# Batch 0 of a packed-attention and ELU-FFN kernel, done by head groups

## The chip, the cores and the metric

The program runs on one core of one Trainium2 chip. The metric is the device time of one execution, in microseconds (us). Engines are named as the profile names them: PE (TensorE matmul; PEld its weight loads), DVE (VectorE), ACT (ScalarE), POOL (GpSimd) and SP (SyncE, which here only issues DMAs). Times of day in this document are us from the start of the profiled execution's span.

## What is computed

```python
def sm_attn(qq, kk, vv):
    s = scale * np.matmul(qq, kk.transpose(0, 1, 3, 2))
    s = s - np.max(s, axis=-1, keepdims=True)
    a = np.exp(s)
    a = a / (np.sum(a, axis=-1, keepdims=True) + 1e-09)
    return np.matmul(a, vv)
p_packed = sm_attn(p, k, v)
out = sm_attn(q, p_packed, p_packed)
...
h = x @ w_in
g = np.where(h > 0.0, h, alpha * (np.exp(np.minimum(h, 0.0)) - 1.0))
return (g @ w_out).astype(np.float32)
```

There are 8 batches, 8 heads, 576 tokens, 64 columns a head, 32 packed queries a head, and x is the attention's output with the heads side by side (4608 x 512). w_in is 512 x 2048, w_out 2048 x 512, all float32.

## The kernel before, in words

**The work of a batch.** The first attention (packed queries p against k) gives 32 packed values a head. The kernel never forms x: since x is A times the packed values, with A the weights of the second softmax, h is A times M, where M is the packed values times w_in. Heads are kept in two groups g: the even heads (g = 0) lie in partitions 0 to 63 of the inputs, the odd ones (g = 1) in 64 to 127, and four heads of 32 packed queries fill 128 rows. A batch runs through `attention`: scores `s1`, maximum and exponential (`smax1`, `sexp1`), transposes `tr1` and copies out of PSUM, the sums with the values `pv`, division `norm`, a transpose `tr2` whose copy `tr2c` leaves the packed values in `ppT`, then for each of two cuts of the tokens the second softmax: scores `s2`, and on DVE `fold` (a 32x32 transpose), `smax`, `ssub`, (ACT `sexp`), `ssum`, `srec` (two small instructions), `smul`, `unfold`. Batch 0 is cut at token 256; its first cut is called the first stretch here.

**M and the products.** `mstep` multiplies `ppT` by 512 columns of w_in in two parts of 256 columns (M part 0 needs blocks 0 and 1 of w_in, part 1 blocks 2 and 3), and ACT or DVE copies the part out of PSUM. A product f (line 1536 for batch 0's first four) multiplies one block of 128 columns of M by the weights A, summed over the two groups; ACT takes it through `relu` and `ex`, DVE through `elu`, `cast` and `sub_own` split it in a high and a low half, and `out_mm` (lines 1658 to 1661) multiplies it by block f of w_out. After these first products PE goes on to products of the same kinds to the end.

**Weights.** Each block of 128 columns of w_in (called i0, i1, ...) or rows of w_out (o0, o1, ...) is loaded by SP as 512 KB, then `top` (a cast on ACT or DVE) and `join` (DVE) turn the loaded words into their float32 form; for w_out `high` and `low` split it further.

**What sets the order.** All work is collected as operations with their dependences. The order in which they are issued, and the engine of each (A, V, G for ACT, DVE, POOL), is written out in a table of numbers, `ORDER`; `PLACES` gives the PSUM banks. Every engine works through its instructions in that order, and one that waits holds up those behind it on its engine. All loads go through SP's one queue. `ONES` gives, by operation, how many extra matmuls (`warm_up`, line 435, on a tile of ones, results unused) PE does behind it; they come to an end before the first product.

Of the kernel before, what the change touches and what calls it, by code (L numbers as in the profile page):

```python
# [10 lines left out]
F32 = mybir.dt.float32  # L11
# [14 lines left out]
0 2 1 7 8 9 10 11 403 404V 405 406V 14 12 416 417V 17 15A 16A 3 4 20 18A 19A 21 13 23A 22A 24 25A  # L26
418 408 5 26 409V 410 400 401A 27 28 29 6 37 48 424 30 425A 402 411 31 32 33 34 529 530A 747 38 39
407G 55 35A 426 412A 413 754 531 748 755 749 40 49 50 56 532A 750 756 751A 414V 757 415G 752G 57 761
41 59 42 758A 759G 43 36 44 419 420A 58 421 753 62 762 763 432 60 65 422V 760 433A 63A 64A 764 768
440 441A 434 442 533 765A 766V 51 61 66A 67V 45 423G 769 534 535 52 770 771 68 69A 435 436A 772V  # L30
773V 775 782 70A 71 437 776 783 767 438V 777 778 72A 551 784 793 427 428A 552 456 439V 785 779A 780G
457A 786A 53 429 430A 431G 557 553 73 794 795 558 458 801 74 75 554 443 444A 787V 796 76 445 802 803
774 797 448 449A 781 450 798V 799G 451 559 77 804 446A 555 447G 806 807A 808G 78 556 810 811 812 813
814 560 561 46A 818 819 820 79 459 788 800 562 80 821 47 54 95 102 789A 805 81 815A 816G 823 84 791A
85 822 452A 453 536 537 824A 827 828 460A 825G 86 87 454A 835 836 837 461 829 455G 840 831 809 830
491 96 817 826 838 538 88 89 832A 833G 82A 83 462A 841A 844 845 90 842V 91 92 504 846 97 852 848 847
463G 505A 499 506 834 843 103 93A 853 94 865 854 492A 849V 850G 855 857 104 858A 106 872 851 866 867
# [12 lines left out]
1013 573 1011 1038A 1045A 115 117A 656G 657G 574 116V 1039V 1046V 658V 540 665V 666G 1031 1048 1049  # L50
1055 1027 1040 1056 1057 1058 1050 655 100 101 142 1051 1032 1062 1069 1052A 663V 664G 659A 660V
1059V 1005 1028 1053V 1063 1060G 1064 1047 1054 1070 1065 661V 662V 667 1066A 1067G 1061 1071 1072
1076 1083 1073A 1074G 1068 1029 1077 1084 1030 669V 1078 541 548 1085 670G 1086 654 1079 549 671V
1080V 1087A 542 543 550 1033 544 1081G 676A 678A 679G 681 677V 672V 118 119A 1088V 1075 673G 1096
1097 1104 120 143 1098 1100 674A 1099 675G 1090 131 1101A 1102G 1113 1082 1105 668 1114 1106 1115
121 122 123 124 125 1109 1089 1103 1110A 144 682G 1107 1116 1117 683V 1118A 1108 1119V 1111V 1121
1122 1123 1124 1130 1126 1127A 684V 689V 1128V 691V 1112 1120 1131 1132 1133 1134 685A 686V 1138
1091 687A 1125 1139 1140 1143 1141 1129 1135A 1136V 1144V 1093 1094 1095 1145G 1147 1155 126 690G
1148 1137 1146 1149 1156 1151 1157 1160 1150 1158 1092 1152A 1153V 127 128 1170 132 133 1161A 1159
1142 688G 1162G 692G 1171 1172 1173 1178 1179 1180 1181 680 1174 1175A 1154 1163 1183 1167 1184A  # L60
1187 1195 695V 1176V 1188 1189 1164 1177 134 1185V 1191 1190 1196 1186 1192A 696G 1182 1168 1169
1193G 1165 1166 1224 697V 698V 135 704V 1197 1200 1194 705G 707 1198 1199 1201A 1204 1212 1202V 1203
1205 1206 699V 700V 701V 1208 1207 1213 1214 1217 1215 1209A 1210V 1218A 1219G 1227 1234 1211 136
137 1228 1229 1230 1241 1235 1236 1237 1220 149 1231A 1232V 1233 138 139 1238A 694 1239G 1242 1243
1244 1225 1248 1245A 1246V 693 702V 703V 708V 709V 1249 706 1250 1251 1255 1256 710V 1257 1258 1252A
1253G 1221 1222 1223 1240 1247 715A 716V 1259A 1260V 717A 711A 712V 713A 714V 719 1262 1269 718V
1283 575 578 1263 1264 1265 721V 722G 720 1270 1271 1226 1272 576 577 1266A 1267V 1276 723V 129A
730A 1254 1261 130 731V 733 728A 729V 724A 725V 726A 727V 581 732 1273A 1274V 734V 579 1289 1286
1268 1275 1277 1278 1279 735G 580 736V 140A 1280A 1281V 737V 1298 738G 1313 582 583 1290 1304 743A
744V 739A 740V 1291 741A 742G 150 152 1292 746 153 154 745 156 157 1305 151 1282 1319 155 1287 584  # L70
1306 1307 1293G 1294G 1284 1295G 1296 1297 1334 1320 141 158 1308V 1309V 1310G 1321 1322 1323V 1324V
1325V 1311 1312 1299 159 162 1326 1327 1335 1336 1337 1338G 145 1339G 1328 1300 1301 1302 1303 1340G
160 1314 164 1349 1315 1316 1343 1350 1317 1318 1351 1352 1353G 1354G 585 1330 1331 586 1355V 1332
1341 1342 1356 1364 1288 1365 1357 1366 1329 1333 1367 1368V 1369V 1370G 1379 1380 1381 1382 1383V
1345 163 1346 1344 1347 1348 1360 1358 1361 165 146 1384V 1385V 1371 1372 1386 1387 1394 1395 166
167 1416 1396 161 1417 1418 1397 1420 1398G 1419 1362 1399V 168 169A 1359 1363 1375 1400V 1421 1373
1388 1401 170V 171 172A 1216 1402 1422 1423 1424 1426 1438 1439 1440 1441 1427G 1428V 1376 1377 1443
1374 1378 1442 1444 1445 1448 1446 147 148 173 1429G 1430 1449G 1450G 174 175 176 1285 1425 1431
# [116 lines left out]
    "623476764764674507501234454664670460126723064647676765045614653204545465456450456120457365777777"  # L195
    "7777032105674333330"
)
ONES = {0: 3, 8: 8, 17: 4, 21: 3, 24: 2, 26: 16, 529: 7}


@with_exitstack
def packed_attention_elu_ffn(
# [22 lines left out]
    nc = tc.nc  # L225
# [1590 lines left out]
```

## Time and profile before

| | us |
|---|---|
| three timed runs | 641.54, 643.30, 643.62 |
| their median | 643.3 |
| the profiled execution | 642.62 |
| its span, first to last instruction | 640.8 |
| PE busy in it | 630.3 |
| DVE busy in it | 534.7 |
| ACT busy in it | 418.9 |
| POOL busy in it | 164.9 |

The profiled execution's time holds 1.8 us around its span. Busy times are of one engine each, and PE's includes the matmuls on ones before the first product.

### The profile page before, as it was taken

To read this page: it belongs to the slowest core of one execution; us is meant where nothing else is said; L and a number is where in the kernel's file an instruction comes from. 1 tells how busy PE (TensorE), PEld (TensorE's weight loads), DVE (VectorE), ACT (ScalarE), POOL (GpSimd) and SP (SyncE) were. 2 spreads that over 40 slices of the span, in tenths; PEclk is the share of its full clock that TensorE was granted. 3 is DMA by queue.
4 is the path that set the end of the run, shared out by engine and by line. 5 is a ranking of instruction groups with operands and counts; after the bars stand their busy time and mean duration, and the time that the engine had idled before them with its cause. 6 is when DMAs were issued, how large, how long until landed. Compare 5 with 4: busy or idle time off the path is not lost.

```text
span 640.8 us, 16120 instructions
## 1 busy us (share of the span) xinstructions
PE 630.3 (98%) x6130; PEld 561.9 (88%) x6130; DVE 534.7 (83%) x1093; ACT 418.9 (65%) x796; POOL 164.9 (26%) x258
## 2 busy tenths in 40 slices
PE   9999999999999999999999999999999999999996
PEld 4567988889789888999989897999889998999996
DVE  3999988779999789878886998898788989667756
ACT  3789987566677657755776577656566667545452
POOL 1224223433232311222123232123111322113121
PEclk9999999999999999999999999999999999999999
DMA  9985795656489978887888989888877777565762
GB/s 346 374 279 197 246 320 166 230 158 225 143 296 307 277 240 280 286 299 231 297 277 276 269 264 317 271 296 301 252 267 272 224 217 245 170 201 189 230 195 82
DMA packets 85405, 160.43 MB, mean 250 GB/s; under 512 B 24272, under 2 KB 40144, under 8 KB 85200
## 3 DMA queue, kind: packets, MB, share of 16 engines
q1 hardware_dynamic: 85040, 158.88, 75.3%
q8 instruction: 48, 0.79, 0.5%
q10 hardware_dynamic: 288, 0.52, 0.2%
q14 instruction: 29, 0.24, 0.1%
HBM read 132.90 MB, written 26.48 MB: 249 GB/s over the span
## 4 chain that ended last, share of the span: by engine, by line
PE 85%; DVE 5%; DMA 5%; ACT 1%; issue 1%; POOL 1%; SPq 0%; DVEq 0%; POOLq 0%; ACTq 0%
PE psum L1426 37%; PE psum L1271 20%; PE psum L1543 6%; PE psum L998 4%; PE psum L1658 4%; PE psum L1661 4%; PE psum L1659 4%; PE psum L435 2%; PE psum L815 2%; DMA kvq<-in_qT 2%; DMA swb<-swb_dram 2%; PE psum L876 1%; DMA out<-part 1%; PE psum L1536 1%; DVE part L1458 1%
## 5 line engine op out<-in xcount | busy, mean ns | idle before, releaser
L1353 POOL TENSOR_TENSOR w<-w 128x128 f32<-128x128 f32 (+1 forms) x167 | 93.8, 565 | 298.5 <-DVE w L1278 77.7
L428 ACT CAST g<-w 128x896 fp32r<-128x896 f32 x96 | 90.0, 940 | 61.2 <-POOL w L1353 28.7
L1361 DVE TENSOR_TENSOR g<-w,g 128x896 fp32r<-128x896 f32 x96 | 104.6, 1092 | 16.6 <-ACT g L428 15.6
L1271 PE MATMUL psum<-a_hi,m_hi 128*128 128x256 f32 (+1 forms) x384 | 112.5, 293 | 0.0
L1271 PE MATMUL psum<-a_lo,m_hi 128*128 128x256 f32 (+1 forms) x384 | 110.2, 287 | 0.0
L1271 PE MATMUL psum<-a_hi,m_lo 128*128 128x256 f32 (+1 forms) x384 | 110.2, 287 | 0.0
L1426 PE MATMUL psum<-wo_b,g 128*128 128x256 f32 x672 | 94.2, 276 | 0.0
L1426 PE MATMUL psum<-wo_a,g 128*128 128x256 f32 x672 | 93.8, 276 | 0.0
L1426 PE MATMUL psum<-swa,g 128*128 128x256 f32 x672 | 93.5, 275 | 0.2 <-DMA swa<-swa_dram 0.2
L1426 PEld LDWEIGHTS psum<-wo_b,g 128*128 128x128 f32 x672 | 84.3, 192 | 4.8 <-issue 4.0
L1426 PEld LDWEIGHTS psum<-wo_a,g 128*128 128x128 f32 x672 | 84.3, 192 | 3.1 <-issue 1.3
L1426 PEld LDWEIGHTS psum<-swa,g 128*128 128x128 f32 x672 | 84.4, 192 | 0.4 <-DMA swa<-swa_dram 0.4
L1271 PEld LDWEIGHTS psum<-a_hi,m_hi 128*128 128x128 f32 x384 | 73.2, 191 | 9.5 <-issue 2.8
L1271 PEld LDWEIGHTS psum<-a_lo,m_hi 128*128 128x128 f32 x384 | 73.3, 191 | 0.1
L1271 PEld LDWEIGHTS psum<-a_hi,m_lo 128*128 128x128 f32 x384 | 73.2, 190 | 0.0
L1283 ACT ACTIVATE e<-psum 128x320 f32<-128x320 f32 x96 | 41.2, 431 | 31.9 <-PE psum L1271 31.3
L1426 PE MATMUL psum<-swb,g 128*128 128x256 f32 x336 | 56.5, 277 | 0.8 <-DMA swb<-swb_dram 0.6
L1426 PEld LDWEIGHTS psum<-swb,g 128*128 128x128 f32 x336 | 46.6, 192 | 3.4 <-issue 2.2
L1278 DVE SCALAR_TENSOR_TENSOR w<-e,psum 128x256 f32<-128x256 f32 x96 | 39.1, 414 | 9.8 <-ACT e L1286 8.4
L1286 ACT ACTIVATE e<-e 128x320 f32<-128x320 f32 x96 | 44.4, 470 | 2.5
L1353 DVE TENSOR_TENSOR w<-w 128x128 f32<-128x128 f32 (+1 forms) x121 | 40.8, 342 | 6.0 <-POOL w L1353 3.8
L1278 DVE SCALAR_TENSOR_TENSOR w<-w,psum 128x512 f32<-128x512 f32 x48 | 32.7, 683 | 13.7 <-ACT w L1286 12.2
(143 smaller groups left out, 1222.5 us busy)
## 6 DMA issues: line engine op xcount, KB each, us to landing
swa<-swa_dram SPq DMA_DIRECT2D x96, 512.0 KB, 5.0
swb<-swb_dram SPq DMA_DIRECT2D x96, 256.0 KB, 4.0
kvq<-in_v SPq DMA_DIRECT2D x16, 640.0 KB, 6.2
raw<-in_w_out SPq DMA_DIRECT2D x16, 511.8 KB, 5.5
raw<-in_w_in SPq DMA_DIRECT2D x16, 511.8 KB, 6.1
kvq<-in_kT SPq DMA_DIRECT2D x14, 576.0 KB, 6.2
kvq<-in_qT SPq DMA_DIRECT2D x14, 576.0 KB, 5.7
out<-part SPq DMA_DIRECT2D x28, 256.0 KB, 4.5
```

The costliest lines, as they stand in the source:

```text
L428: (nc.scalar.copy if e == "ACT" else nc.vector.tensor_copy)(out=out, in_=in_)
L998: nc.tensor.matmul(ps.t[cols_of(pair), g, :w], lhsT=st.ppT.t[rows_of(g), pair, :], rhs=w_in_sb[rows_of(g), pair, c * FC + part * w:c * FC ...
L1271: nc.tensor.matmul(ps, lhsT=m_b[p].t[:, g, o:o + P], rhs=in_turn(st.a.t[q][:, g, cols]), start=(n == 0), stop=(n == 3 * G - 1),)
L1278: nc.vector.scalar_tensor_tensor(out=out, in0=e_, scalar=-1.0, in1=ps, op0=ALU.add, op1=ALU.max)
L1283: nc.scalar.activation(out=out, in_=ps, func=AF.Relu, scale=-1.0)
L1286: nc.scalar.activation(out=x, in_=x, func=AF.Exp, scale=-1.0)
L1353: eng(e).tensor_tensor(out=out, in0=x, in1=y, op=o)
L1361: nc.vector.tensor_tensor(out=g_b.all[:, 7 * P:(7 + b1 - b0) * P], in0=blocks(b0, b1), in1=g_b.all[:, :(b1 - b0) * P].bitcast(F32), op=ALU ...
L1426: nc.tensor.matmul(a.t[:, at * H:(at + rhs.shape[1]) * H], lhsT=operand(blk, p), rhs=rhs, start=new and n == k == 0, stop=a.final == (u, m ...
L1543: nc.tensor.matmul(ps_b.t[:, :n_tok], lhsT=m_b[x].t[:, g, o:o + P], rhs=in_turn(st.a.t[y][:, g, cols]), start=(n == 0), stop=(n == 3 * G - 1),
L1658: nc.tensor.matmul(a.t, lhsT=g_b.t[0][:, t], rhs=w[0], start=first, stop=False)
L1659: nc.tensor.matmul(a.t, lhsT=g_b.t[0][:, t], rhs=w[1], start=False, stop=False)
```

## The change

Batch 0 is worked through by head groups. Its loads of k, of the values and of the first stretch of q come one per group, k and q as 64 partitions each; the host lays the values out so that each of their two loads holds one group. Scores, transposes back to `ppT`, the first stretch's softmax, both parts of the first M and the first four products are operations of one group. The DVE steps of the first stretch then work on 256 elements a partition instead of 512, twice as many of them. The scaling of p goes from POOL to ACT. The whole of `ORDER`, `PLACES` and `ONES` is new (731 PE operations of the change stand in an order that differs from before in places throughout); two lines of `ORDER` are shown, and what it does at three places is shown below.

```diff
-0 2 1 7 8 9 10 11 403 404V 405 406V 14 12 416 417V 17 15A 16A 3 4 20 18A 19A 21 13 23A 22A 24 25A
...
+0 2 1 9A 10 418 419A 420 421A 5 11 13 12 18 14 15 19A 20V 423 424V 425 426 16 17 21 22A 3 6 24 23A
+427A 428 429V 26A 4 25 27A 7 28 29A 32 430G 422G 33 34 35 30 31A 41 36 42 43 44 37 415 416A 417 38
+39 40 8 63 70 45 46 47 52 48 49 544 439 545A 440A 546 431 766 547A 767 768 441 769 53 54 774 770 775
...
-ONES = {0: 3, 8: 8, 17: 4, 21: 3, 24: 2, 26: 16, 529: 7}
+ONES = {13: 3, 18: 1, 21: 3, 24: 3, 28: 2, 30: 2, 52: 8, 544: 1}
...
+    BY_G = [0]
+    F_BY_G = 4
...
+            if b in BY_G:
+                n = P if c < 4 else S - 4 * P
+                return v_b[h % 2].t[:n, c * E // 2 + h // 2 * D:c * E // 2 + (h // 2 + 1) * D]
...
         def load_k(e, n):
             if b == 0:
-                nc.sync.dma_start(out=k_b[0].t, in_=kT[b])
+                nc.sync.dma_start(out=k_b[0].t[rows_of(n)], in_=kT[b, rows_of(n)])
...
         def load_q(e, n):
-            if b == 0:
-                cs = CUTS[n]
+            if b == 0 and n < G:
+                cs = CUTS[0]
+                nc.sync.dma_start(
+                    out=q_b[0].t[rows_of(n), :, cs], in_=qT[b, rows_of(n), :, cs]
+                )
+            elif b == 0:
+                cs = CUTS[1]
                 nc.sync.dma_start(out=q_b[0].t[:, :, cs], in_=qT[b, :, :, cs])
...
-        for name, fn, bufs, t in (
+        if b == 0:
+            lds = {x: [] for x in "kvq"}
+            for name, n in (("k", 0), ("v", 0), ("q", 0), ("k", 1), ("v", 1), ("q", 1), ("q", 2)):
+                fn, bufs = dict(k=(load_k, k_b), v=(load_v, v_b), q=(load_q, q_b))[name]
+                x = bufs[n % len(bufs)]
+                prev_ld = op(
+                    -60, {"DMA": {"k": 1.47, "v": 1.48, "q": 1.64 if n == 2 else 0.65}[name]},
+                    lambda e, fn=fn, n=n: fn(e, n), take=[x] if n < len(bufs) else [],
+                    after=lds[name][-1:], lag=-1.9,
+                )
+                if n >= len(bufs):
+                    x.users.append(prev_ld)
+                lds[name].append(prev_ld)
...
+        def s1_g(e, g):
+            for half in range(2):
+                for pair in range(NPAIR):
+                    nc.tensor.matmul(
+                        ps1[g].t[cols_of(pair), half, :HS], lhsT=p_b.t[rows_of(g), pair, :],
+                        rhs=keys(pair)[rows_of(g), half * HS:(half + 1) * HS],
+                        start=True, stop=True,
+                    )
...
+        scaled = op(t - 1, {"ACT": 0.27, "DVE": 0.24} if SCALE_ON != "POOL" or b in BY_G else {"POOL": 0.53}, scale, [ld_p], use=[p_b])
+        if b in BY_G:
+            o1 = o = None
+            for g in range(G):
+                o1 = op(
+                    t, {"PE": 1.0}, lambda e, g=g: s1_g(e, g), [ld_k[g], scaled],
+                    take=[ps1[g], e1s[g]], use=[p_b] + k_b, after=[free, o1], mode=1,
+                )
+                o = op(t, {"DVE": 0.76}, lambda e, g=g: smax1(e, g), [o1], use=[ps1[g]], after=[o])
+                o4s.append(op(
+                    t, {"ACT": 0.84}, lambda e, g=g: sexp1(e, g), [o], use=[ps1[g], e1s[g]],
+                ))
...
-                ts[2], {"PE": 0.65}, lambda e: pv(e, [0]), ld_v + tr_done[:2], take=[ps, pp_b],
+                ts[2], {"PE": 0.65}, lambda e: pv(e, [0]), ld_v[:1] + tr_done[:2], take=[ps, pp_b],
...
-                ts[2], {"PE": 0.65}, lambda e: pv(e, [1]), tr_done[2:], use=[ps, pp_b] + v_b + e1T[1:],
+                ts[2], {"PE": 0.65}, lambda e: pv(e, [1]), ld_v[1:] + tr_done[2:], use=[ps, pp_b] + v_b + e1T[1:],
...
+        if b in BY_G:
+            st.ppT_g, o = [], None
+            for g in range(G):
+                o = op(
+                    ts[3], {"PE": 0.03}, lambda e, g=g: tr2_g(e, g), [done[g]],
+                    take=[] if g else [pt2, st.ppT], use=[pp_b] + ([pt2, st.ppT] if g else []),
+                    lag=0.07, after=[o],
+                )
+                st.ppT_g.append(op(
+                    ts[3], {"ACT": 0.27, "DVE": 0.29}, lambda e, g=g: tr2c_g(e, g), [o],
+                    use=[pt2, st.ppT], after=st.ppT_g[-1:],
+                ))
+            st.ppT_op = st.ppT_g[1]
...
+                st.af_g, p_s, p_m, p_u, p_v = [], None, None, None, None
+                for g in range(G):
+                    n = lambda fn, g=g: lambda e: fn(e, g)
+                    o = p_s = st.s2_op = op(
+                        t, {"PE": us(0.51)}, n(s2_g), [lds["q"][g], st.ppT_g[g]],
+                        take=[] if g else [ps, t1], use=[q_b[0], st.ppT] + ([ps, t1] if g else []),
+                        mode=1, after=[p_s],
+                    )
+                    o = op(t, {"DVE": of(0.77)}, n(fold_g), [o], use=[ps, t1])
+                    o = p_m = op(t, {"DVE": of(0.75)}, n(smax_g), [o], use=[t1], after=[p_m])
+                    o = op(t, {"DVE": of(0.76)}, n(ssub_g), [o], use=[t1], two=True)
+                    o = op(t, {"ACT": of(0.69)}, n(sexp_g), [o], use=[t1])
+                    o = p_u = op(t, {"DVE": of(0.75)}, n(ssum_g), [o], use=[t1], after=[p_u])
+                    o = op(t, {"DVE": 0.36}, n(srec_g), [o], two=True)
+                    o = op(t, {"DVE": of(0.75)}, n(smul_g), [o], use=[t1], two=True)
+                    o = p_v = op(
+                        t, {"DVE": of(0.77)}, n(unfold_g), [o], take=[] if g else [t2],
+                        use=[t1] + ([t2] if g else []), after=[p_v],
+                    )
+                    st.af_g.append(o)
+                prev = list(st.af_g)
+                st.af_done.append(o)
...
     def mstep(b, c, part, parts_, prio, deps=(), also=False):
         st = sts[b]
+        if b in BY_G and c == 0:
+            return mstep_g(b, c, part, parts_, prio)
...
+        fl = [c * 4 + part * 4 // parts_ + n for n in range(4 // parts_)]
+        o = None
+        for g in range(G):
+            o = op(
+                prio, {"PE": 0.46}, lambda e, g=g: mm(e, g), [w_ready[True, f] for f in fl] + [st.ppT_g[g]],
+                after=[o], take=[] if g else [ps] + (m_b if part == 0 else []),
+                use=[st.ppT] + ([ps] if g else []) + (m_b if part or g else []), mode=1,
+            )
+            st.m_g[part, g] = op(
+                prio, {"ACT": 0.33, "DVE": 0.38}, lambda e, g=g: hi(e, g), [o], use=[ps] + m_b,
+            )
+        st.m_done[c, part] = st.m_g[part, 1]
...
+        if by_g:
+            x1 = None
+            for hg in range(G):
+                x1 = op(
+                    i, {"PE": 0.434}, lambda e, g=hg, mm_g=mm_g: mm_g(e, g),
+                    [st.m_g[f % 4 // 2, hg], st.af_g[hg]], take=[] if hg else [ps_b],
+                    use=m_b + [a_b] + ([ps_b] if hg else []), after=[x1, run.get(("h", hg))],
+                )
+                run["h", hg] = x1
+                if first_dense is None:
+                    first_dense = x1
+                    warm_b.users.append(x1)
+                home_op.deps.append(x1)
```

On SP, the loads at the start of the program, before. The names are the tiles written; raw_175 is o0, raw_188 i2, raw_264 i1, raw_295 i0, raw_314 i3, raw_319 o1, and the two kvq are the values.

```order
L584 DMA k0_139<-in_kT 128x2304
L605 DMA p_141<-in_pT 128x128
L459 DMA raw_175<-in_w_out 128x2047
L459 DMA raw_188<-in_w_in 128x2047
L592 DMA kvq_203<-in_v 128x1280
L592 DMA kvq_205<-in_v 128x1280
L459 DMA raw_264<-in_w_in 128x2047
L597 DMA q0_266<-in_qT 128x4x256
L459 DMA raw_295<-in_w_in 128x2047
L597 DMA q0_266<-in_qT 128x4x320
L459 DMA raw_314<-in_w_in 128x2047
```

The same place with the change, where the two loads of p are left out, and raw_150 is o0, raw_184 i1, raw_188 o1, raw_293 i0, raw_335 i3, raw_343 i2 and raw_358 o2.

```order
L591 DMA k0_136<-in_kT 64x2304
...
L463 DMA raw_150<-in_w_out 128x2047
L591 DMA k0_136<-in_kT 64x2304
L463 DMA raw_184<-in_w_in 128x2047
L463 DMA raw_188<-in_w_out 128x2047
L599 DMA kvq_205<-in_v 128x1280
L599 DMA kvq_207<-in_v 128x1280
L604 DMA q0_239<-in_qT 64x4x256 x2
L463 DMA raw_293<-in_w_in 128x2047
L609 DMA q0_239<-in_qT 128x4x320
...
L463 DMA raw_335<-in_w_in 128x2047
L463 DMA raw_343<-in_w_in 128x2047
```

The second half of k stands behind o0, a load of w_out (o1) has come ahead of the values, and i2 has gone from fourth place to the end of the batch's loads, behind i3.

On PE, from the sums with the values to the first products, before: `pv` is line 815, `tr2` 851, `s2` 876 (256 and 320 tokens), M 998, products 1536; the matmuls on ones between them are left out.

```order
L815 MATMUL psum<-kvq,tmp 32x64 x40
...
L851 MATMUL psum<-ident,pp 128x128
...
L876 MATMUL psum<-q_266,ppT 32x256 x8
...
L876 MATMUL psum<-q_266,ppT 32x320 x8
L998 MATMUL psum<-w_in_sb,ppT 32x256 x8
...
L1536 MATMUL psum<-k_326,m_hi 128x256 x4
L637 MATMUL psum<-kvq,p 32x288 x16
```

With the change the same steps are lines 866, 911, 1019 and 950, 1197 and 1791; the second row of `pv` is group 1's.

```order
L866 MATMUL psum<-kvq_205,tmp_173 32x64 x20
L866 MATMUL psum<-kvq_207,tmp_195 32x64 x20
L911 MATMUL psum<-ident,pp 64x128
...
L1019 MATMUL psum<-q_239,ppT 32x256 x4
L911 MATMUL psum<-ident,pp 128x128
...
L950 MATMUL psum<-q_239,ppT 32x320 x8
...
L1197 MATMUL psum<-w_in_sb,ppT 32x256 x4
...
L1791 MATMUL psum<-k_300,m_hi 128x256 x4
L1197 MATMUL psum<-w_in_sb,ppT 32x256 x8
L654 MATMUL psum<-kvq,p 32x288 x16
```

Group 0's `tr2` stands behind group 1's `pv`, and M part 0 behind the second cut's scores (line 950) and the eight matmuls on ones that follow them. Part 1 of M (x8) still stands between the first two products and the scores of batch 1 (line 654).

On ACT with the change, from the copies of M part 0 (m_hi) on; line 1755 is `relu`, 1761 `ex`, and the raw numbers are those above.

```order
L432 COPY m_hi_329<-psum_102 128x256
L432 CAST tops_121<-raw_335 128x512
L1755 ACTIVATE e_348<-psum_102 128x256
L1761 ACTIVATE e_348<-e_348 128x256
L432 CAST tops_121<-raw_358 128x512
L432 CAST a_hi_363<-k0_300 128x2x256
L432 CAST tops_121<-raw_343 128x512
L1755 ACTIVATE e_369<-psum_102 128x256
```

The `top` of i3 comes between the copies of the two groups' M, and the `top` of i2 behind the first product's `relu` and `ex`, the `top` of o2 and a cast of A. Before, i2's `top` was on DVE, ahead of `srec1`.

## Rows read from the trace of the kernel before

**Rows 1.** Stretches: busy us of each engine, granted clock, DMA share, GB/s.
```profile
10.00:16.00 6.00, 6.00 (x117) 3.35 (x118) 3.46 (x9) 2.82 (x9) 0.00 (x0) 1.00 1.03 397
22.00:28.20 6.20, 4.72 (x62) 3.09 (x60) 6.17 (x11) 5.53 (x14) 3.04 (x5) 1.00 0.95 330
240.00:634.00 394.00, 393.63 (x3945) 368.87 (x3944) 324.15 (x634) 249.66 (x424) 93.47 (x164) 1.00 0.77 250
634.00:640.80 6.80, 1.21 (x11) 1.02 (x10) 2.76 (x6) 0.00 (x0) 0.00 (x0) 0.80 0.42 155
```

**Rows 2.** PE's waits: what waited, for whom, total us, times, longest.
```profile
PE psum L1658 <- ACT tmp L654: 1.5, 1, 1.5
...
PE psum L876 <- DMA kvq<-in_qT: 0.8, 2, 0.5
```

**Rows 3.** PE's timeline, 12 to 29 us: start, us, instruction, count.
```profile
12.19 1.73 PE L815 MATMUL psum<-kvq,tmp 128*32 128x64 f32 x80
...
14.58 0.33 PE L851 MATMUL psum<-ident,pp 128*128 128x128 f32 x1
...
15.27 0.66 PE L876 MATMUL psum<-q,ppT 64*32 64x256 f32 x16
15.87 3.63 PE L435 MATMUL psum<-part 128*128 128x512 bf16 x16
19.43 0.77 PE L876 MATMUL psum<-q,ppT 64*32 64x320 f32 x16
...
22.08 1.89 PE L1536 MATMUL psum<-k,m_hi 128*128 128x256 f32 x8
23.90 0.66 PE L998 MATMUL psum<-w_in_sb,ppT 64*32 64x256 f32 x16
24.36 1.29 PE L637 MATMUL psum<-kvq,p 64*32 64x288 f32 x32
...
28.25 0.48 PE L1658 MATMUL psum<-wo_a,g 128*128 128x512 f32 x1 [1.53 <-ACT tmp L654]
```

**Rows 4.** Issues of two loads on SP, and those loads: KB, us to landing.
```profile
3.37 0.49 SPq L592 DMA_DIRECT2D kvq<-in_v  x1
...
6.36 0.57 SPq L597 DMA_DIRECT2D q<-in_qT  x1
...
kvq<-in_v SPq DMA_DIRECT2D x1, 640.0 KB, 8.6
...
q<-in_qT SPq DMA_DIRECT2D x1, 640.0 KB, 12.6
```

**Rows 5.** DVE's timeline, 16 to 26 us.
```profile
16.11 0.72 DVE L887 STREAM_TRANSPOSE tmp<-psum 128x512 f32<-128x512 f32 x1 [1.57 <-PE psum L876]
...
18.19 0.68 DVE L477 SCALAR_TENSOR_TENSOR w_in_sb<-raw,tops 128x512 uint32<-128x512 uint32 x1
...
19.69 0.17 DVE L912 TENSOR_SCALAR sm<-sm 128x16 f32<-128x16 f32 x1
...
20.91 0.71 DVE L929 STREAM_TRANSPOSE k<-tmp 128x512 f32<-128x512 f32 x1
...
25.06 0.41 DVE L1570 SCALAR_TENSOR_TENSOR e<-e,psum 128x256 f32<-128x256 f32 x1
```

**Rows 6.** ACT's timeline, 20 to 25 us.
```profile
20.41 0.77 ACT L428 CAST tops<-raw 128x512 f16<-128x512 bf16 x1 [1.47 <-DMA raw<-in_w_in]
...
21.66 0.62 ACT L428 CAST a_hi<-k 128x512 fp32r<-128x512 f32 x1
...
24.29 0.41 ACT L1567 ACTIVATE e<-e 128x256 f32<-128x256 f32 x1
```

**Rows 7.** Stores from 32 partitions: issue on SP, then the first's and last's landing.
```profile
261.93 3.76 SPq L752 DMA_DIRECT2D turn_dram<-tmp  x8
...
turn_dram<-tmp SPq DMA_DIRECT2D x1, 80.0 KB, 3.3
...
turn_dram<-tmp SPq DMA_DIRECT2D x1, 80.0 KB, 1.8
```

More of the change, by code (lines that the diff above doesn't have):

```diff
@@ L657, in sexp1, with srec1_g @@
             )
+        def srec1_g(e, g):
+            if g == 0:
+                sv["ri"] = small.tile([P, G], F32, tag="ri", name="ri")
+            x = sv["ri"][:, g:g + 1]
+            nc.vector.tensor_scalar(
+                out=x, in0=sv["sm"][:, g:g + 1], scalar1=EPS, scalar2=None, op0=ALU.add
+            )
+            nc.vector.reciprocal(out=x, in_=x)
         def srec1(e):
@@ L734, in attention @@
                 ))
-        o5 = op(ts[1], {"DVE": 0.36}, srec1, o4s)
+        if b in BY_G:
+            o5s = []
+            for g in range(G):
+                o5s.append(op(ts[1], {"DVE": 0.3}, lambda e, g=g: srec1_g(e, g), [o4s[g]], after=o5s[-1:], two=True))
+        else:
+            o5s = [op(ts[1], {"DVE": 0.36}, srec1, o4s)] * G
         if b >= TURNED:
@@ L856, in tr2c, with tr2_g, tr2c_g @@
             copy(e, st.ppT.t.rearrange("p c i -> p (c i)"), ps.t[:, :P])
-        o = op(ts[3], {"PE": 0.03}, tr2, done, take=[pt2, st.ppT], use=[pp_b], lag=0.07)
-        st.ppT_op = op(ts[3], {"ACT": 0.27, "DVE": 0.29}, tr2c, [o], use=[pt2, st.ppT])
+        def tr2_g(e, g, ps=pt2):
+            n = (g + 1) * D
+            nc.tensor.transpose(
+                out=ps.t[:n, :P], in_=pp_b.t.rearrange("p g d -> p (g d)")[:, :n], identity=ident
+            )
+        def tr2c_g(e, g, ps=pt2):
+            copy(e, st.ppT.t.rearrange("p c i -> p (c i)")[rows_of(g)], ps.t[rows_of(g), :P])
+        if b in BY_G:
+            st.ppT_g, o = [], None
[10 more added lines that the diff above has]
+            st.ppT_op = st.ppT_g[1]
+        else:
+            o = op(ts[3], {"PE": 0.03}, tr2, done, take=[pt2, st.ppT], use=[pp_b], lag=0.07)
+            st.ppT_op = op(ts[3], {"ACT": 0.27, "DVE": 0.29}, tr2c, [o], use=[pt2, st.ppT])
         st.a_done, st.af_done = [], []
@@ L941, in attention, with s2_g, part_g, in_g @@
             x = w / HS
+            def s2_g(e, g, ps=ps, w=w, half=half):
+                for pair in range(NPAIR):
+                    nc.tensor.matmul(
+                        ps.t[cols_of(pair), g, :w], lhsT=st.ppT.t[rows_of(g), pair, :],
+                        rhs=queries(pair, half)[rows_of(g)], start=True, stop=True,
+                    )
+            def part_g(g, t1=t1, w=w):
+                return t1.t.rearrange("p c k -> p (c k)")[:, g * w:(g + 1) * w]
+            def in_g(g, part_g=part_g):
+                return part_g(g).rearrange("p (n i) -> p n i", i=NPK)
@@ L1792 @@
     values = np.concatenate([values, last.reshape(B, 128, 2, E // 2).transpose(0, 2, 1, 3)], 3)
+    values[0] = first.reshape(5, 128, 2, 4 * D).transpose(2, 1, 0, 3).reshape(2, 128, 5 * 4 * D)
     arrays = {
```

428 lines of the change are left out of this document (244 added, 184 removed).

## The prediction, made before the changed kernel ran

> **What bounds the kernel now.** I read four views, in this order. The stretches by window say which engine sets the time: from 240 to 634 us PE is busy 393.63 of 394 us, and already from 22 us on it is short of work for little more than 1.5 us in a piece [rows 1]. So what is behind the first products is a fixed amount of PE work, and the end moves by as much as the front moves; only a wait of PE counts. PE's waits come next: the longest behind the start is the 1.5 us ahead of the first output product, the others together are small [rows 2]. Third, PE's timeline shows the front: sums with the values at 12.19, scores of the first stretch at 15.27, products at 22.08, M part 1 at 23.90, the first output product at 28.25 [rows 3]. I measure the change at this last place, since PE is dense behind it. Fourth, what feeds the front: the loads run at 397 GB/s in one stream with nothing idle between them, and DVE is busy 6.17 of 6.2 us between 22 and 28.2 [rows 1]. A step that is earlier only in its own engine's order gains nothing when its load or DVE is the later one; that is the test to put to each part of the change.
>
> **The change, part by part.**
>
> *Sums with the values.* Before, the second load of values was issued at 3.37 and landed 8.6 us later, at 12.0 [rows 4], and PE began at 12.19. Now o1, 512 KB, stands ahead of the values, and i1 where i2 was; k, p, o0 and the values are the same bytes. 512 KB at 397 GB/s are 1.3 us [rows 1], so group 1's values land at 13.3. Group 0's come 1.6 us before them, but that doesn't help: in PE's order its `tr2` stands behind group 1's `pv`. That takes half of 1.73, so group 0 gets to `tr2` at 13.35 + 0.87 = 14.2. From `tr2` to `s2` it was 14.58 to 15.27, 0.7, and from `s2` to the first DVE step 15.27 to 16.11, 0.84 [rows 3, 5]. Group 0's first `fold` thus starts at 15.75, 0.35 earlier than before, and with half the data. What group 0 gained in k's half load, in scores and exponential is spent waiting here; I cost it at nothing, and its cover is this wait for the values.
>
> *The first stretch on DVE.* Before, the chain ran from 16.11 to 20.91 + 0.71 = 21.62 [rows 5]. Now there are twelve steps of 256 elements instead of six of 512. No row has these steps at 256, but another DVE instruction of 256 took 0.41, where full ones took 0.7; bounds are 0.35 (half) and 0.7 (no saving), and I take 0.41 and 0.03 for the handover. 12 x 0.44 = 5.3; two pairs of `srec` at slightly under the 0.5 that separate 19.69 from its successor, 0.9; the `join` of i0 in between, 0.6 [rows 5]. Group 0 and 1 alternate, so ACT's exponentials lie beside DVE. Chain: 15.75 + 6.75 = 22.5 for group 1. The split makes it 0.9 later than before, not earlier.
>
> *M part 0.* It now stands behind the second cut's scores and eight matmuls on ones. The second cut's q is behind the same bytes as before. By the stream's rate it lands at 13.3 + 1.70 MB / 397 GB/s = 17.6; before, it was issued at 6.36 and landed after 12.6, at 19.0 [rows 4]. Scores 0.77 and eight times 3.63/16 = 0.23 give M part 0 at 20.2 or 21.6 [rows 3]. At 20.2 both groups of M and their copies are ready at about 22.5, even with the `top` of i3 (0.77, at 20.41 or later [rows 6]) between the copies, and are hidden under the DVE chain. I take the early landing, since it is bytes of one stream that runs at that rate; the late one is a rival below.
>
> *First products.* The first one's second group starts at 22.5, and behind it three quarters of 1.89 end at 23.9 [rows 3], where they ended before, at 22.08 + 1.89 = 23.97. The gain is nil.
>
> *M part 1.* It needs i2, which was early and now is last. Its `top` stands on ACT behind `relu`, `ex`, the `top` of o2 and a cast of A. The first product is out at 22.5 + 0.47 + 0.2 = 23.2; 0.41 + 0.41 + 0.77 + 0.7 + 0.77 = 3.1 (`relu` and the cast of A, which have no row here, at the price of `ex` and of a full-width step) [rows 5, 6] make 26.3, the `join` on DVE 0.7 more: M part 1 starts at 27.0. DVE by itself, with two `join`s, `fold` and `smax` of the second cut, an `elu` and a subtraction behind the chain, would allow 26.8, so both engines are at their limit. PE then has M part 1 by groups (2 x 0.46, as M's 0.66 overlaps what follows it: 23.90 to 24.36), batch 1's scores, 1.29, the third product and half of the fourth, 3 x 0.47 [rows 3]: 3.6, so the first output product starts at 30.6. Half a product, 0.47, is work that stood behind it before. 30.6 - 0.47 - 28.25 = **1.9 us later**. The 1.5 us wait for a bank of PSUM is gone, but a wait of 3.1 ahead of M part 1 takes its place.
>
> *The rest.* The matmuls are the same. PE waits twice for a later batch's q, 0.8 in all [rows 2]; PE being later, I let 0.2 of it go. The new order further on I cost at nothing, with 1 us either way: PE is dense there, so there is little to win, and what a wait could cost is the size of those in [rows 2].
>
> **The sum.** +1.9 - 0.2 = +1.7 on the profiled execution's 642.6: 644.3. That execution lies 0.7 under the median of the runs, so the median would go from 643.3 to **645.0**, +0.26%. A measurement of this kernel can tell about 0.3% (1.9 us) from no change: this is just inside.
>
> **The loads of 64 partitions.** Stores from 32 partitions, eight of 80 KB issued over 3.76 us, landed from 265.2 (3.3 after the first issue) to 267.0 (1.8 after the last, at about 265.2): seven in 1.8 us, 319 GB/s [rows 7]. So narrow transfers need not be slow, though these are stores; no row has a load into 64 partitions. By these rows I cost the halves at their bytes.
> The Trainium skill speaks against this: its page "SBUF — State Buffer", section "Door 1: The DMA port swizzle", says that 64 partitions reach only 8 of the 16 DMA ports, and gives 196 GB/s for 64 partitions against 328 for 128 at 1 MiB. By that page the half loads would each take nearly twice as long, which is the second rival's time; the stores above, the trace's only narrow transfers, don't agree with it.
>
> **Rivals.**
> - *The late q (slower).* The second cut's q lands at 19.0 again. M part 0 at 21.6, its second group's copy, behind i3's `top`, done at 24.0, the first product 1.5 later than in my sum: +3.2, 645.8 in the profile, 646.5 by the median. It decides from a landing at 18 on. For it: that load's own row. Against it: it is bytes in a stream. The wait of 3.1 us could also lower the granted clock, which was 1.00 through the 1.5 us one and 0.80 on average over the last 6.8 us, most of which PE idles [rows 1]; 3.6 us of work at half rate would add up to 3.6.
> - *Half loads at half rate (slower).* Loads of 1.7 MB (k and the first stretch's q) take 1.7 MB / 397 GB/s = 4.3 us more, of which 3.0 are ahead of the values: sum +1.7 + 4.3, 648.6, median 649.3. For it: no load row excludes it; against it: [rows 7].
> - *M part 1 is not late (faster).* If its inputs are in place when the first products end, as before, M part 1 starts at 24.2, the first output product at 27.8, and less 0.47 that is 0.9 before 28.25. With the waits of [rows 2] behind it gone and DVE's half steps at 0.35 (1.1 earlier) it comes to about -2.5: 640.1, median 640.8. It takes over from M part 1 at 24.4 and earlier. Against it: the order of ACT's instructions.
> - *The change does not do what it says.* Group 0 gets no lead, since PE's order and the values' landing hold it; this is part of my sum, and alone gives 642.6 and 643.3.
>
> **Chances and range.** Within 0.3%: 0.42 (my sum, down to no effect). Slower: 0.41, of it 0.33 for the late q and a front 0.3 or more worse than summed, 0.08 for half rate. Faster: 0.17. For 8 in 10 I cut the half-rate case's far end and the best of the faster one: 641.0 to 648.2. The middle case alone is 643.5 to 646.
>
> **What would show it.** In the changed kernel's profile: group 1's values landing at 13.3 and `tr2` of group 0 only behind the second `pv`; first `fold` at 15.75, last `unfold` ending at 22.5; first products ending at 23.9; a wait of PE of 3 us ahead of M part 1 at 27.0, released by a DVE `join`; the first output product at 30.6; PE dense behind it. The prediction is wrong if M part 1 starts at 25 or before, if a k half takes as long as k did (the second half landing behind 9 us), or if the new order opens or closes waits of over 1 us far behind the front.

## The result and the profile after

The changed kernel takes 650.18 us (median of 4 runs, 649.70 to 652.01), the kernel before 643.13 beside it (641.54 to 643.62): the ratio is 1.0122, 95% interval 1.0105 to 1.0139. It is slower by 7.0 us, where the sum said +1.7 and its range ended at 648.2. The profiled execution took 650.43 us with a span of 648.7. Two single executions far off the rest of their kernel, one of the kernel before (919 us) and one of a changed one (1302 us), are left out of the ratios below.

Stretches of the changed kernel, in the columns of [rows 1], and under them the first stretch of the kernel before:

```profile
0.00:10.00 10.00, 5.52 (x27) 1.80 (x27) 0.71 (x3) 2.56 (x4) 1.58 (x7) 0.89 0.81 187
10.00:16.00 6.00, 4.61 (x24) 2.30 (x26) 1.69 (x4) 2.56 (x6) 0.00 (x0) 0.50 1.01 383
240.00:634.00 394.00, 392.51 (x3930) 367.31 (x3929) 325.19 (x646) 252.73 (x428) 93.05 (x163) 1.00 0.77 252
634.00:648.70 14.70, 9.16 (x83) 8.97 (x81) 8.77 (x15) 2.62 (x4) 1.10 (x1) 0.91 0.24 89
```
```profile
0.00:10.00 10.00, 8.83 (x55) 3.23 (x56) 2.05 (x5) 2.46 (x5) 2.11 (x8) 1.00 0.83 315
```

Nearly as in [rows 1], PE is dense from 240 to 634 (1.1 us less busy), and the difference is work left behind 634: 9.16 us of PE instead of 1.21. So most of the loss comes from the front, and the first two rows say where: in the first 10 us the loads bring 187 GB/s with the DMA engines busy 0.81 of the time, where the kernel before has 315 GB/s with them busy 0.83, and from 10 to 16 us the granted clock is 0.50 (the 1.2 GHz level), where it was 1.00 before.

PE's timeline of the changed kernel, to hold against [rows 3]:

```profile
6.94 1.45 PE L664 MATMUL psum<-k,p 64*32 64x288 f32 x16 [1.70 <-ACT p L737]
11.29 2.15 PE L664 MATMUL psum<-k,p 64*32 64x288 f32 x16 [2.90 <-DMA k<-in_kT]
...
14.62 1.27 PE L834 MATMUL psum<-ident,tmp 128*128 128x128 f32 x5
...
19.89 0.90 PE L866 MATMUL psum<-kvq,tmp 128*32 128x64 f32 x40
20.72 0.30 PE L911 MATMUL psum<-ident,pp 128*64 128x128 f32 x1
...
23.74 1.90 PE L439 MATMUL psum<-part 128*128 128x512 bf16 x8
25.78 0.64 PE L1197 MATMUL psum<-w_in_sb,ppT 64*32 64x256 f32 x8
...
28.80 1.53 PE L1791 MATMUL psum<-k,m_hi 128*128 128x256 f32 x6 [0.88 <-DVE k L1067]
33.03 0.67 PE L1197 MATMUL psum<-w_in_sb,ppT 64*32 64x256 f32 x16 [2.70 <-DVE w_in_sb L481]
33.49 1.18 PE L654 MATMUL psum<-kvq,p 64*32 64x288 f32 x32
34.60 1.56 PE L1791 MATMUL psum<-k,m_hi 128*128 128x256 f32 x6
35.81 0.57 PE L1874 MATMUL psum<-wo_a,g 128*128 128x512 f32 x1
```

PE has group 0's scores at 6.94 and then waits for group 1's half of k until 11.29. From there everything is late: the second `pv` at 19.89, M part 0 at 25.78, M part 1 at 33.03 behind a wait of 2.70 for a DVE `join`, the first output product at 35.81 instead of 28.25.

The loads behind it, in the columns of [rows 4]: k's two halves and group 1's values on SP, and their landings.

```profile
0.72 0.60 SPq L591 DMA_DIRECT2D k<-in_kT  x1
...
2.46 0.51 SPq L591 DMA_DIRECT2D k<-in_kT  x1
...
4.67 0.67 SPq L599 DMA_DIRECT2D kvq<-in_v  x1
```
```profile
k<-in_kT SPq DMA_DIRECT2D x1, 576.0 KB, 5.6
...
k<-in_kT SPq DMA_DIRECT2D x1, 576.0 KB, 8.8
...
kvq<-in_v SPq DMA_DIRECT2D x1, 640.0 KB, 12.4
```

The first half lands at 6.3, the whole of k only at 11.3, and group 1's values at 17.1, not at 13.3; the second cut's q lands at 22.6. In the kernel before, the whole of k took no longer than the first half does here:

```profile
k<-in_kT SPq DMA_DIRECT2D x1, 1152.0 KB, 5.2
```

DVE's part of the front is as it was summed (against [rows 5]): the first `fold`, the last `unfold`, then the `join` of i2 that M part 1 waits for.

```profile
22.16 0.45 DVE L1034 STREAM_TRANSPOSE tmp<-psum 128x256 f32<-128x256 f32 x1 [2.34 <-PE psum L1019]
...
28.21 0.45 DVE L1067 STREAM_TRANSPOSE k<-tmp 128x256 f32<-128x256 f32 x1
...
32.30 0.68 DVE L481 SCALAR_TENSOR_TENSOR w_in_sb<-raw,tops 128x512 uint32<-128x512 uint32 x1
```

### The profile page after: what moved, and what is told of

Read it like the earlier page. It is cut to its first block, busy times and chain, and to the rows that moved or that the text cites. A ratio compares the mean times of both kernels' runs of the same rounds, so it can differ in the third digit from the quotient of the medians.

```text
span 648.7 us, 16107 instructions
## 1 busy us (share of the span) xinstructions
PE 630.0 (97%) x6108; PEld 561.6 (87%) x6111; DVE 535.9 (83%) x1111; ACT 422.6 (65%) x798; POOL 161.7 (25%) x252
## 5 line engine op out<-in xcount | busy, mean ns | idle before, releaser
L1547 POOL TENSOR_TENSOR w<-w 128x128 f32<-128x128 f32 (+1 forms) x155 | 89.1, 577 | 291.8 <-DVE w L1547 111.7
L1555 DVE TENSOR_TENSOR g<-w,g 128x896 fp32r<-128x896 f32 x96 | 104.8, 1094 | 13.3 <-ACT g L432 12.3
L1547 DVE TENSOR_TENSOR w<-w 128x128 f32<-128x128 f32 (+1 forms) x133 | 44.2, 333 | 8.8 <-POOL w L1547 6.2
L1477 ACT ACTIVATE w<-psum 128x512 f32<-128x512 f32 x48 | 28.7, 598 | 25.6 <-PE psum L1465 12.5
```

What stands on the lines that cost most here:

```text
L1477: nc.scalar.activation(out=out, in_=ps, func=AF.Relu, scale=-1.0)
L1547: eng(e).tensor_tensor(out=out, in0=x, in1=y, op=o)
L1555: nc.vector.tensor_tensor(out=g_b.all[:, 7 * P:(7 + b1 - b0) * P], in0=blocks(b0, b1), in1=g_b.all[:, :(b1 - b0) * P].bitcast(F32), op=ALU ...
```

## The experiments

The theory that the result suggests: loads into 64 partitions take nearly twice as long for their bytes, and PE's wait for k lets the clock fall, which makes what follows later still. The first rival: the loss is in the new order of the instructions. The chips of these runs scatter more than the first one (before: medians of 643.9 to 644.3, single runs mostly from 641 to 648), so each kernel is held against the runs of before on its own chip (the us given are differences of medians), and differences under about 1.5 us are not told apart.

### Are narrow loads slow?

The kernel before, with k in two loads of 64 partitions:

```diff
-                nc.sync.dma_start(out=k_b[0].t, in_=kT[b])
+                for g in range(2):
+                    x = slice(64 * g, 64 * g + 64)
+                    nc.sync.dma_start(out=k_b[0].t[x], in_=kT[b, x])
```

> The kernel before, with nothing changed but that batch 0's k comes in two loads of 64 partitions, one right behind the other. Theory (half rate, one behind the other): the first half lands at about 6.4, the second at 10.5 to 11.2 instead of 5.96 for the whole, the values 4 to 5 us later than 12.0, and the time is 646.5 to 649. Rival (the two halves go into different partitions and run beside each other): both land by 6.5 and the time is 643.1, unchanged. Rival (one more DMA costs only its issue): 643.1 to 643.6.

The same with two loads of all 128 partitions (`x = slice(2 * g, 2 * g + 2)`, `k_b[0].t[:, x]`, `kT[b, :, x]`):

> The kernel before with batch 0's k in two loads that each fill all 128 partitions with half the columns. Theory (what costs is the 64 partitions and not the division): both land by 6.3, the values at 12.0 to 12.4, and the time is within 0.1% of before. Rival (a second load costs about 2.8 us by itself): the values land at 14.4 as with two loads of 64 partitions, and the time is 0.5% or more above before.

Measured: the narrow halves 648.01 us, ratio 1.0067 (1.0042 to 1.0091), +3.8 us; the wide halves 642.63, ratio 1.0000 (0.9974 to 1.0026). Landings of the two loads of k, issued at 0.72 and 1.36 in the first kernel, 0.72 and 1.16 in the second:

```profile
k<-in_kT SPq DMA_DIRECT2D x1, 576.0 KB, 5.4
...
k<-in_kT SPq DMA_DIRECT2D x1, 576.0 KB, 7.4
```
```profile
k<-in_kT SPq DMA_DIRECT2D x1, 576.0 KB, 3.7
...
k<-in_kT SPq DMA_DIRECT2D x1, 576.0 KB, 4.8
```

The second half lands 8.8 - 6.1 = 2.7 us behind the first where it is narrow (576 KB, 0.22 MB per us) and 6.0 - 4.4 = 1.6 us where it is wide. It is the 64 partitions and not the division, and two narrow loads in one queue don't run beside each other, although they go to different partitions. That alone costs the kernel before half of what the change lost. The second half was expected at 10.5 us or later and came earlier, but the time is in the range expected. What follows is later by about as much as the whole of k (8.8 instead of 5.9): the first `fold` starts at 18.82 instead of 16.11, the first output product at 30.97 instead of 28.25. The granted clock is 1.00 in this kernel where the changed one has 0.50, so this loss needs no lowered clock:

```profile
10.00:16.00 6.00, 5.95 (x113) 3.24 (x102) 4.35 (x10) 3.02 (x8) 0.00 (x0) 1.00 1.02 409
```

### The changed kernel with whole loads

```diff
-                nc.sync.dma_start(out=k_b[0].t[rows_of(n)], in_=kT[b, rows_of(n)])
+                if n == 0:
+                    nc.sync.dma_start(out=k_b[0].t, in_=kT[b])
```

> The changed kernel with batch 0's k in one load of 128 partitions again; q still comes in halves and everything else is as changed. Theory (loads into 64 partitions run at half rate, and PE's wait for the second half of k lowers the clock behind it): k lands before 6.5 instead of 11.24, group 1's values at about 13.5 instead of 17.11, PE's wait of 2.9 us for k is gone, the granted clock between 10 and 16 us is 0.9 or more instead of 0.50, the first fold is at about 16 instead of 22.16, and the time is 644.5 to 646. Rival (the loss is in the new order of the instructions, of which the front's waits are only a symptom): it stays at 649 or more.

The first stretch's q whole as well, in the same manner:

> The changed kernel with k and the first stretch's q each in one load of 128 partitions; everything else by groups as changed. This is the case that the prediction's sum was made for: group 1's values land at about 13.3, first fold at 15.75, M part 1 at 27, the first output product at 30.6, the time at 645.0. Theory (half rate): a little under the kernel with k alone whole, by up to 1 us, since the loads behind q come 0.7 us earlier. Rival (q's halves cost nothing): the same as that kernel within 0.3 us. Rival (the order): 649 or more.

Measured: k whole 647.81, ratio 1.0054 (1.0019 to 1.0089), between the ranges of the theory and of its rival; k and q whole 646.28, ratio 1.0032 (1.0012 to 1.0052), +2.1 us; before 644.18. The changed kernel itself on a second chip:

> The changed kernel once more, unaltered, so that the kernels run beside it have it on their own chip. Both theories: 7 us above the kernel before on the same chip, 1.0105 to 1.0139 of it.

It took 649.95, ratio 1.0097 (1.0066 to 1.0128). So whole loads give back 4 to 5 of the 6 to 7 us. The 2.1 that are left are near the sum's 1.7, but not by its steps: in the kernel with both whole, group 1's values are issued at 3.81 and land at 13.1, as summed, and the first `fold` still starts at 18.20, not 15.75. PE, DVE and the load of that kernel:

```profile
10.66 0.82 PE L834 MATMUL psum<-ident,tmp 128*128 128x128 f32 x5 [2.26 <-ACT tmp L680]
...
15.94 0.90 PE L866 MATMUL psum<-kvq,tmp 128*32 128x64 f32 x40
```
```profile
8.29 0.69 DVE L481 SCALAR_TENSOR_TENSOR mi<-raw,tops 128x512 uint32<-128x512 uint32 x1 [7.17 <-ACT tops L432]
8.90 1.42 DVE L674 TENSOR_REDUCE mx<-psum 128x1 f32<-128x576 f32 x2
```
```profile
kvq<-in_v SPq DMA_DIRECT2D x1, 640.0 KB, 9.3
```

The `join` of o0 stands ahead of the first maximum on DVE and waits for o0's cast; so the transposes are at 10.66, and the second `pv` at 15.94, 2.8 us behind the landing of its values.

### Is the clock a cost of its own?

The changed kernel with PE kept at work while it waits for k: `ONES` gets `10: 12` (operation 10 is group 0's scores).

> The changed kernel with 12 more matmuls on ones in PE's order behind group 0's first scores, so that PE works while it waits for the second half of k; the loads are as changed. Theory (the lowered clock is a cost of its own behind the late landing): k's second half lands at about 11.2 as before, the granted clock between 10 and 16 us rises from 0.50 to 0.8 or more, group 1's scores take 1.5 us or less instead of 2.15, the transposes 0.7 instead of 1.27, the first fold comes 1 to 2.6 us earlier, and the time is 647.5 to 649. Rival (only the landings count): 650.2, unchanged.

It took 651.22, ratio 1.0111 (1.0073 to 1.0149), without a profile that shows places. A second time:

> The changed kernel with 12 more matmuls on ones behind group 0's first scores, a second time: the first time gave 651.2 us but a profile of an execution that was slowed twofold throughout, which shows no place. Theory (the lowered clock is a cost of its own): the granted clock between 10 and 16 us is 0.8 or more instead of 0.50, and the first fold starts 1 us or more before 22.16. Rival (only the landings count): fold at 22.16 within 0.4. By the time of the first run, the changed kernel's own within 0.5 us, I expect the clock to rise, the scores and transposes to be shorter, and the fold to be held by something else, which this profile should name.

653.34, ratio 1.0143 (1.0107 to 1.0178), beside 1.0097 for the changed kernel on that chip. Its stretches and PE:

```profile
10.00:16.00 6.00, 5.30 (x76) 2.81 (x75) 3.12 (x9) 4.05 (x9) 0.00 (x0) 1.00 1.01 390
...
22.00:28.20 6.20, 4.52 (x24) 1.27 (x24) 3.62 (x11) 0.42 (x1) 0.53 (x1) 0.56 1.03 415
```
```profile
11.04 1.17 PE L664 MATMUL psum<-k,p 64*32 64x288 f32 x16 [0.31 <-DMA k<-in_kT]
...
23.68 1.32 PE L950 MATMUL psum<-q,ppT 64*32 64x320 f32 x16 [3.21 <-DMA q<-in_qT]
24.94 3.60 PE L439 MATMUL psum<-part 128*128 128x512 bf16 x8
28.46 1.08 PE L1197 MATMUL psum<-w_in_sb,ppT 64*32 64x256 f32 x8
```

The clock is 1.00 where it was 0.50, group 1's scores take 1.17 instead of 2.15, and the first `fold` starts at 19.35 instead of 22.16. The end gains nothing: the second cut's q lands at 23.6 (22.6 in the changed kernel), M part 0 stands behind its scores, and now the clock falls there, so that eight matmuls on ones take 3.60 instead of 1.90. The next run puts M part 0 ahead of that wait (544 and 546 ahead of 52 in `ORDER`, ones `10: 12`, `41: 4`, `52: 4`):

> The changed kernel with its narrow loads, the 12 more matmuls on ones behind group 0's first scores, and on PE M part 0 ahead of the second cut's scores. Theory (the lowered clock costs 2.5 to 3 us in front of the first fold; the run with the ones alone gave nothing because PE then waited 3.2 us for the second cut's q with M part 0 behind it, and the clock fell there): the wait no longer holds M part 0, the first products start at about 26 instead of 30.4, and the time is 2 us or more below the changed kernel's. Rival (the late loads of i3 and i2, at 25.5 and 26.8, hold M part 1 in any case): the wait ahead of M part 1 grows by what the front gains and the time stays within 1 us of the changed kernel's.

651.42, ratio 1.0117 (1.0071 to 1.0163), with single runs from 647.03 to 654.05: no gain that can be told. In its profile M part 0 is at 22.68 and the first products at 27.13, but M part 1 waits 2.70 for the same `join` and starts at 31.72. So the low clock costs time in the front and is not shown to cost anything at the end. That the late landings and the chain to M part 1 hold the end as long as the loads are narrow is what these waits suggest; no run takes them apart.

### What holds the kernel with whole loads

Four runs change the order of that kernel. First, the cast, `join` and high half of o0 (419, 420, 421) behind the first attention's copies:

> The changed kernel with k and the first stretch's q in whole loads, and o0's cast, join and high half behind the first attention's exponentials and copies instead of ahead of the first maximum. Theory (with whole loads, DVE's first maximum is held by the join of o0, which waits for o0's landing at 7.4; this makes the transposes late, lets the clock fall, and so the sums with the values run 2.5 us behind their landing): the first maximum starts at 7.7 instead of 8.9, the first transpose at 9.5 instead of 10.66, the granted clock between 10 and 16 is above 0.72, the sums with group 1's values start at 13.2 instead of 15.94, the first fold at 15.3 to 15.8 instead of 18.2, and the time is 1.5 to 2.5 us below the kernel with whole loads alone: within 0.2% of the kernel before. Rival (the values' landing and PE's order hold it anyway): no change against whole loads alone, 2 us above before.

Then also the cast of i2 (432) behind 547 and its `join` (433) behind 441:

> The same, and the cast of i2 on ACT right behind the copies of M part 0 and its join on DVE right behind that of i3, instead of behind the first product's two activations, the cast of o2 and the high half of A. The loads are as in the run with o0 later. Theory (M part 1 waits for i2 in ACT's and DVE's order and not for its load): the wait of 2 to 3 us ahead of M part 1 shrinks to 0.3 to 1, and the time falls by another 1.5 to 2.5 us, to 0.1 to 0.4% under the kernel before. Rival (i2's load lands too late to matter, or the second cut's softmax, now later, holds the next products): less than 0.5 us.

646.48, ratio 1.0042 (1.0018 to 1.0065), and 645.72, ratio 1.0027 (1.0007 to 1.0047). The second, on PE and DVE:

```profile
13.44 0.90 PE L866 MATMUL psum<-kvq,tmp 128*32 128x64 f32 x40
...
18.81 0.77 PE L950 MATMUL psum<-q,ppT 64*32 64x320 f32 x16 [1.85 <-DMA q<-in_qT]
...
26.55 0.66 PE L1197 MATMUL psum<-w_in_sb,ppT 64*32 64x256 f32 x16
27.26 1.21 PE L654 MATMUL psum<-kvq,p 64*32 64x288 f32 x32
31.00 1.56 PE L1791 MATMUL psum<-k,m_hi 128*128 128x256 f32 x6 [2.54 <-DVE m_hi L432]
```
```profile
15.84 0.45 DVE L1034 STREAM_TRANSPOSE tmp<-psum 128x256 f32<-128x256 f32 x1 [0.47 <-PE psum L1019]
...
16.78 1.45 DVE L1042 TENSOR_TENSOR tmp<-tmp,mx 128x256 f32<-128x256 f32 x1
```

The first `fold` is at 15.84, where the sum had it, and it was at 16.04 with o0 alone moved, so the place of o0 on DVE was what held it. The wait ahead of M part 1 is gone too. Each time the next wait takes the time back: the second cut's q (landing at 18.8, the late case of the prediction), then M part 1's copies on DVE behind the second cut's steps. The third run orders these and moves POOL's low halves away (544 and 546 ahead of 52; 549 and 551 on DVE ahead of 54; 430 and 422 behind 49), the fourth also puts o1's load (426) behind i2's:

> The last kernel (whole loads, o0 later, i2 earlier) with the order at the front changed again: on PE M part 0 ahead of the second cut's scores, with the matmuls on ones divided between the two places; on DVE the copies of M part 1 directly behind the fold of the second cut; on POOL the low halves of o0 and o1 behind the first stretch's last unfold. Theory (with whole loads what is left is order: a wait of 1.9 us for the second cut's q, one of 2.5 for M part 1's copies, and one DVE subtraction of 1.45 instead of 0.42 while POOL works beside it): all three go, the first products start at about 21.5 instead of 24.48 and the first output product at about 27.5 instead of 32.21; the time is 2 to 4 us below that kernel's, 642 to 643.5 if before is at 644. Rival (the end is held by something behind the front): less than 1 us.

> The same, and the load of o1 behind that of i2 instead of ahead of the values, its cast, join and halves in the places that o2's had. Theory (o1 ahead of the values costs its 512 KB at the stream's rate): group 1's values land at 12.0 instead of 13.3, the first fold 1.3 us earlier, and the time is 0.3 to 1.3 us below the kernel beside it, since part of it is held by the later loads. Rival (the front is then held by the later loads of i0, q and i2 alone): no change.

646.39, ratio 1.0038 (1.0014 to 1.0062), and 647.96, ratio 1.0072 (1.0042 to 1.0103). In the fourth the first output product is at 27.30, ahead of before's 28.25, and PE then waits 3.8 us for batch 1's exponential, behind o2's cast on ACT, where my order had put it. The last pair mends that, and adds the narrow loads to the same order:

> Whole loads of k and q with the front's order mended where the last two runs showed new waits: o2's cast, join and high half behind batch 1's exponentials instead of ahead of them; o0's low half on POOL before the first stretch begins, where DVE is idle, and o1's behind the second subtraction; the subtractions of the first two products on POOL ahead of DVE's second-cut subtraction. Theory (what is left above before with whole loads is these waits alone): the 3.8 us wait for batch 1's exponential and the 1.2 us wait for the first product's low half go, the two joins ahead of M part 1 take 1.4 instead of 2.2 to 3.2, the first output product starts at 26.5 to 27.3, and the time is 1 to 2 us below before, 0.997 to 0.9985. Rival (the work by groups loses as much further on): equal to before or up to 2 us above, with the first output product at 27 and new waits behind it.

> The same kernel with k and the first stretch's q in halves of 64 partitions again, as in the change. Theory (the narrow loads cost what their landing costs, in any order of the instructions): k's second half lands at 11 instead of k at 6, group 1's values at 15.5 to 16 instead of 12.6, the first fold 3.5 to 6 us later, and the time is 3 to 6 us above the kernel beside it. Rival (the loss of the change was order, and the landings are covered once the order is right): less than 1.5 us above.

Whole loads 646.85, ratio 1.0032 (1.0006 to 1.0059); narrow 652.76, ratio 1.0125 (1.0098 to 1.0153), on one chip: the narrow loads cost 5.9 us in this order. These 5.9 include whatever a lower clock costs: from 10 to 16 us the granted clock is 0.50 with the narrow loads and 1.00 with the whole ones. PE of the first of the two, and the waits that follow:

```profile
26.81 0.57 PE L1874 MATMUL psum<-wo_a,g 128*128 128x512 f32 x1
```
```profile
PE psum L834 <- ACT tmp L680: 2.4, 2, 1.8
...
PE psum L1158 <- ACT tmp L432: 1.9, 1, 1.9
PE psum L866 <- ACT tmp L432: 1.3, 1, 1.3
```

The first output product is 1.4 us earlier than before, and then ACT's steps of batch 1 hold PE for 1.8 + 1.9 + 1.3 us. None of these five orders with whole loads gained the time that was expected of it. No version tried is faster than before; all with whole loads lie 1.6 to 3.7 us above it. Whether some order makes the division by groups pay is not settled.

## Why the prediction was wrong

**The step that failed** is the costing of k's and q's halves "at their bytes". It rested on the stores of [rows 7], and their 319 GB/s is a misreading: the stores were under way together, so the time between their landings is not the time in which their bytes moved. From the first landing to the last the DMA engines moved 145 GB/s in all, 0.26 MB, where the seven stores hold 0.57 MB:

```profile
265.20:267.00 1.80, 1.80 (x15) 1.80 (x15) 1.06 (x2) 1.77 (x4) 0.66 (x1) 1.00 0.55 145
```

The rows thus had no narrow transfer at the full rate, and nothing in them spoke against the rival. What the runs show in place of "at their bytes" is 0.22 MB per us for 64 partitions. The prediction's own sign of being wrong, a second half landing behind 9 us, came true at 11.3. The second rival had the mechanism and the size: 1.7 + 4.3 gave 649.3; measured 650.2, and the narrow loads measured by themselves 3.8 (k alone, in the kernel before), 4 to 5 (the change against whole loads) and 5.9. That it came so near is partly luck, since its 1.7 is (below). It was given 0.08.
The Trainium skill had spoken against the step, in "SBUF — State Buffer", section "Door 1: The DMA port swizzle": 64 partitions reach half of the ports. This case's trace agrees, by the 0.22 MB per us of the narrow half of k. The page gives 196 GB/s for 64 partitions at 1 MiB.

**Sums with the values: failed for a second reason.** The sum let the values' landing cover whatever comes before it. From the landing of group 1's values to the first `fold` it had 15.75 - 13.3 = 2.45; in the changed kernel it is 22.16 - 17.1 = 5.1, and with whole loads 18.20 - 13.1 = 5.1 too. In the first, k at 11.3 and the low clock hold the transposes; in the second, o0's `join` ahead of the first maximum. With o0 out of the way the `fold` is at 15.84, as summed. I had read PE's and SP's order there, and not DVE's.

**The first stretch on DVE: right.** 6.75 summed, 28.21 + 0.45 - 22.16 = 6.50 measured.

**M part 0 and the late q: both landings occur.** The second cut's q was taken to land at 17.6, and with both loads whole, the sum's own case, it did (issued at 6.24, 11.4 us); in the first two of the other orders, where PE came to wait for it, it landed at 19.1 and 18.8, the rival's case. Why it differs is open. While the `fold` is late it costs nothing.

**M part 1: right in mechanism and size.** From the last `unfold` to M part 1 the sum had 27.0 - 22.5 = 4.5; measured 33.03 - 28.66 = 4.4, with a wait of 2.70 released by the `join` of i2, behind `relu`, `ex`, o2's cast and A's on ACT. Taking i2 out of that order removed the wait.

**From M part 1 to the first output product** 3.6 was summed, 35.81 - 33.03 = 2.8 measured: the scores of batch 1 and the products overlap more than in my rows. **The rest** of the program, costed at -0.2 with 1 us either way, is 9.16 - 1.21 - (35.81 - 28.25 - 0.47) = +0.9.

**The sum for whole loads** came out at +1.7 against +2.1 measured, but partly by chance: its early `fold` was wrong by 2.45 there, the wait of M part 1 is shorter for it (1.9), and the first output product is at 32.39, not 30.6.

## What to carry to other kernels

Price a transfer by a row that covers the same number of partitions in one load, and take a rate from the bytes that moved in a stretch, not from the landings of transfers that were under way together. Splitting a load so that one half can be worked on early doesn't make the half early if it is narrow: k's first half landed no sooner than the whole. And where a stall is taken away, read the order of each of the engines behind it, since the next wait was there in every one of six orders tried.

## What the runs showed of the hardware

POOL and DVE hold each other up in instructions that read two tensors. With i2 earlier, the subtraction of 256 elements at 16.78 above took 1.45 us instead of 0.42 to 0.43 while POOL had two TENSOR_TENSORs of o0's and o1's low halves (15.46 to 17.95, the first line); the reduction just ahead of it, which reads one tensor, took its usual 0.42 beside them (the second). In the third order of those four, two `join`s took 3.19 us beside the same work of POOL (the third), and POOL's took 2.95 instead of 2.49 there; 1.25 is the time of two `join`s with POOL at rest, in the best order (the fourth).

```profile
15.46 2.49 POOL L495 TENSOR_TENSOR wo_a<-mi,wo_a 128x512 fp32r<-128x512 f32 x2 [13.32 <-DVE wo_a L432]
```
```profile
16.32 0.42 DVE L1039 TENSOR_REDUCE mx<-tmp 128x8 f32<-128x256 f32 x1
```
```profile
22.60 3.19 DVE L481 SCALAR_TENSOR_TENSOR w_in_sb<-raw,tops 128x512 uint32<-128x512 uint32 x2
```
```profile
21.77 1.25 DVE L481 SCALAR_TENSOR_TENSOR w_in_sb<-raw,tops 128x512 uint32<-128x512 uint32 x2
```

The Trainium skill's page "SBUF — State Buffer", section "SBUF: two separate sides", says so: the two share a port pair that one instruction holds to its end, and a DVE instruction with two inputs in SBUF takes it against one of POOL that reads SBUF.
